# The same steps of an attention and feed-forward kernel in another order

## The chip, the core and the metric

The kernel runs on one core of one Trainium2 chip. Times are device microseconds of one launch. The core has five instruction queues that run beside each other: TensorE (PE, with the weight loads PEld shown apart), VectorE (DVE), ScalarE (ACT), GpSimd (POOL) and SyncE (SP). The last two, and ScalarE at the very end, also issue DMAs. Every queue runs its own instructions strictly in order; across queues they wait for each other by semaphores.

## The reference

A gated linear attention with a running state is followed by a bilinear feed-forward layer. Batch 4, 8 heads, 768 steps, head size 48; all in float32.

```python
for t in range(S):                       # per batch and head
    state = alpha[t][:, None] * state + outer(k[t], v[t])
    y[t] = q[t] @ state
x = y.transpose(0, 2, 1, 3).reshape(B * S, H * D)        # 3072 x 384
out = ((x @ w_a) * (x @ w_b)) @ w_out                    # w_a, w_b: 384 x 1536
```

`w_a` and `w_b` are drawn at random like the other inputs.

## The kernel before

**Chunks.** The work is cut into six chunks (0 to 5). A chunk is two of the four batches, called units u = 0 and 1, times 256 steps; chunks 0 and 1 are the first 256 steps of the two batch pairs, 2 and 3 the next, 4 and 5 the last. Each chunk goes through three stages.

*Preparation.* `ld` loads a (alpha), k, q and v. `ln` takes the logarithm of alpha on ScalarE; `l2`, `l2s`, `R`, `H` and `L` add pairs of steps and split the sums in parts that TensorE can multiply; `B`, `A2` or `AQ` sum them along time by a triangular matrix; `E` takes the exponentials of the sums (`b`: decay, `i`: its inverse); `ra` and `lv` bring the two steps of a pair to one level; `mk` and `mq` write the scaled keys and queries. `dk`, `de` (first chunks) or the DMAs `dr`, `dl` make the decay of the state. `C` and `Ce` turn keys and queries on TensorE and copy them out of PSUM in chunks 0 and 1; later `T`, a transposing DMA on SyncE, and the copy `Tr` do this.

*Attention.* `v` and `vs` lay out the values. `K` and `K2` (L760, L773) form key-value products, `k` (L787 to L791) updates the state, `D` (L805) forms scores, `M` masks them, or `Mc` copies and `Mm` masks afterwards. `SB` and `SA` (L834) add what the state carries over, `Y` (L834) what lies inside the chunk, and `X` (L870, L872) copies the result out.

*Feed-forward.* `a f` and `b f` (L889) are one of twelve 128-column blocks of x @ w_a and x @ w_b: three matmuls of 512 columns for both units (`*`), or of 256 columns for one. `as` (L895) copies the `a` block out of PSUM on ScalarE, into one of three buffers; `pr` (L903) multiplies it with the `b` block on VectorE. `o m h` (L911) is half h of the product with w_out for output tile m; `oc` (L922) does the same for half of the columns. `ot` (L926 on ScalarE, L928 on VectorE) copies the tile out of PSUM, into one of four buffers that are taken in turn, and `st` (L944) stores it by a DMA of SyncE. `W` and `Wo` load the weights in slices by GpSimd DMAs (`W a`, `W b`: w_a, w_b).

**Where the order comes from.** The order is written out in a string, `PROGRAM`, and nothing reorders it. A step is a name with arguments, and ahead of a line stands the chunk it belongs to: in `1: ot 1 V`, tile 1 of chunk 1 is copied out by VectorE. The last letter of many steps says which engine takes it: V VectorE, S ScalarE, P GpSimd, Y SyncE. The last number of a matmul step is the PSUM bank, 0 to 7, where its result goes (`D`, `SB`, `B` and `AQ` take two neighbours). This loop builds the instructions:

```python
    for line in PROGRAM.split("\n"):
        if line.strip():
            c, ops = line.split(":")
            for op in ops.split(";"):
                name, *args = op.split()
                OPS[name](chunks[int(c)], *args)
```

So the position of a step in the string is its position in its engine's queue. A step waits for what it reads, and for the last use of the bank or buffer that it writes. The buffer of an output tile is the one that `ot` took four calls earlier, and the new `ot` waits until the store out of it has landed:

```python
    def ff_out(ch, m, eng):
        ch.ot[m] = wk.tile([128, d_model], F32, name="ot", bufs=4)
        evict(ch.ot[m], ch.pf["o", m], eng)
```

Chunks overlap: while chunk c is in the feed-forward stage, chunk c + 1 is prepared and goes through attention between the feed-forward blocks. The prediction writes steps with the chunk ahead where it is needed, so `0 st 2` is the store of tile 2 of chunk 0.

Of the kernel before, what the change touches and what calls it, by code (L numbers as in the profile page):

```python
# [72 lines left out]
0: cz 1 v P
1: v 0 S
0: as 11 *; c3 P
1: vs 0 1 S
0: b 11 * 1; pr 11 *; b 6 * 2; pr 6 *
# [174 lines left out]
3: b 8 * 1
2: ot 1 V
3: a 8 * 0; as 8 *
5: l2s 1 P
3: a 6 * 2; as 6 *
5: l2s 0 V; ra 0
3: a 2 * 3; a 9 * 0; as 9 *; b 6 * 2
4: T 0; dr
5: l2 0 P  # L260
3: a 3 * 4; pr 8 *
4: vs 1 0 S
5: R 0; R 1; ra 1
4: Tr 0 V; v 0 S
3: pr 6 *
5: lv 1 q P
3: b 9 * 5; pr 9 *; a 1 * 0; b 2 * 1; as 2 *
4: T 1
3: pr 2 *
5: AQ 6; E 1 i  # L270
4: dl; D 0 0 2; M 0 0
3: as 1 *
5: E 0 i
3: as 3 *; b 1 * 5; pr 1 *; a 5 * 1; as 5 *
# [9 lines left out]
3: pr 3 *
4: D 0 1 0
1: st 1 Y
4: vs 0 1 V; D 1 1 4
5: E 1 b
4: D 1 0 6; Mc 1 0
# [3 lines left out]
4: K * 0 2; k * 0 V; M 0 1
5: dr
2: o 3 1 -; ot 3 S
4: vs 0 0 V
3: b 10 * 6; b 4 * 7; pr 4 *
2: st 1 Y
3: b 5 * 2; pr 5 *
4: SB 1 0; SB 0 4  # L300
5: mq 0 V
4: Mm 1 0 V
3: a 7 * 3; as 7 *; a 10 * 7; as 10 *
2: st 3 Y
4: vs 1 1 S
3: o 3 0 2; o 2 0 3; pr 10 *
4: Y 0; SA 0; X 0 S; Mm 1 1 V
5: mk 0 V
# [1 line left out]
4: SA 1; Y 1; X 1 S  # L310
5: T 0; mk 1 V; T 1; v 0 S
3: b 7 * 6; o 0 0 7
4: b 3 * 0
5: vs 0 1 S
3: pr 7 *
4: b 4 * 1
# [5 lines left out]
5: Tr 0 V
4: pr 6 *; as 8 *; b 8 * 3
5: v 1 V; vs 1 1 V
4: pr 8 *; a 0 * 5; as 0 *; a 7 * 6; as 7 *
3: o 3 1 -; ot 3 S; ot 0 V
5: D 0 0 0; Tr 1 V; Mc 0 0; D 1 0 6
4: pr 0 *
5: M 1 0; D 1 1 4; K * 0 3; k * 0 V
3: o 1 0 2; o 1 1 -  # L330
4: a 11 * 3
5: Mc 1 1; SB 0 0; Mm 1 1 V
3: ot 1 V
4: as 11 *
5: D 0 1 4; M 0 1; SB 1 6
4: b 7 * 2; pr 7 *; a 10 * 3; as 10 *
3: st 2 Y
4: b 11 * 4; pr 11 *; a 2 * 2; b 2 * 3; b 1 * 4; a 5 * 5
# [4 lines left out]
5: vs 1 0 S; vs 0 0 P; Mm 0 0 V; Y 0; SA 0; X 0 V
4: as 5 *
5: Y 1
4: b 5 * 3; pr 5 *; b 10 * 5; pr 10 *
5: X 1 S; a 3 * 0; b 10 * 1; b 3 * 3; a 0 * 5; as 0 *
# [721 lines left out]
```

## Time and profile before

| | us |
|---|---|
| median of 3 runs | 191.82 (191.68 to 191.87) |
| the profiled execution | 191.33 |
| its span, first to last instruction | 189.5 |
| TensorE busy | 183.1 (97%) |
| VectorE busy | 135.3 (71%) |
| ScalarE busy | 117.2 (62%) |
| GpSimd busy | 57.7 (30%) |
| granted TensorE clock | 1.00 throughout |

The page lists busy time, the span in 40 slices of 4.7 us each, the chain of waits that ended last, and the costliest groups of instructions with their mean duration. A wait is listed as who waited, for whom, the total, how often and the longest. A timeline row is the start, the duration, the engine, the line, the operation, the tiles and their shapes, and how many instructions were merged; in brackets stands the idle time before it and what ended it. A DMA row of an issuing queue shows how long the issue took, and the DMA view adds the time from issue to landing.

### The profile page before, as it was taken

How to read it: one execution, taken by the hardware profiler on the slowest of the kernel's cores; microseconds unless marked ns; L12 is line 12 of the kernel's file. 1: busy time of each engine (PE TensorE's matmuls, PEld its weight loads, DVE VectorE, ACT ScalarE, POOL GpSimd, SP SyncE). 2: the span in 40 equal slices, each digit the busy share in tenths (PEclk: the TensorE clock that was granted, in tenths of full speed). 3: DMA queues.
4: the chain of work that ended last, by engine and by line, in shares of the span. 5: the costliest groups of instructions: out<-in, count | busy, mean ns of one | idle time of the engine just before them, and what ended most of it. 6: DMA issues, size and time to landing. Idle time of an engine off the chain costs nothing.

```text
span 189.5 us, 6112 instructions
## 1 busy us (share of the span) xinstructions
PE 183.1 (97%) x2597; PEld 114.6 (60%) x2613; DVE 135.3 (71%) x246; ACT 117.2 (62%) x220; POOL 57.7 (30%) x81
## 2 busy tenths in 40 slices
PE   7999899999999999999999999999999999999993
PEld 3888676656688776644457544646446454545563
DVE  2477778679898999797899898995287753144511
ACT  4497586896978996667475979747625524320610
POOL 8999177985154000203930226002000000000000
PEclk9999999999999999999999999999999999999999
DMA  5999999999999799988999396926902100002123
GB/s 130 265 223 199 263 241 248 237 258 268 236 220 194 102 190 263 266 231 154 208 267 206 93 159 134 127 85 71 175 27 83 45 3 0 0 5 83 42 83 125
DMA packets 64475, 29.41 MB, mean 155 GB/s; under 512 B 55760, under 2 KB 62816, under 8 KB 64448
## 3 DMA queue, kind: packets, MB, share of 16 engines
q1 hardware_dynamic: 46080, 16.34, 40.9%
q0 software_dynamic: 18224, 12.58, 38.8%
q8 instruction: 20, 0.33, 0.7%
q10 hardware_dynamic: 144, 0.10, 0.2%
q14 instruction: 7, 0.06, 0.1%
HBM read 25.98 MB, written 4.74 MB: 162 GB/s over the span
## 4 chain that ended last, share of the span: by engine, by line
PE 88%; DMA 4%; DVE 3%; issue 2%; POOL 2%; ACT 1%; POOLq 0%; ACTq 0%
PE psum L889 47%; PE psum L911 24%; PE psum L834 6%; DMA a_t<-in_alpha_dram 4%; PE psum L805 2%; PE psum L704 2%; PE psum L599 1%; DVE prod L903 1%; PE psum L922 1%; PE psum L773 1%; PE psum L760 1%; PE psum L666 1%; PE psum L557 1%; PE psum L558 1%; DVE vx L928 1%
## 5 line engine op out<-in xcount | busy, mean ns | idle before, releaser
L889 PE MATMUL psum<-xT,wb_t 128*128 128x512 bf16 (+1 forms) x261 | 54.7, 335 | 1.1 <-DVE vx L928 0.4
L889 PE MATMUL psum<-xT,wa_t 128*128 128x512 bf16 (+1 forms) x264 | 54.7, 336 | 0.4 <-issue 0.2
L911 PE MATMUL psum<-wo_t,prod 128*128 128x384 bf16 x276 | 49.2, 326 | 0.1
L889 PEld LDWEIGHTS <-wa_t 128*128 128x128 bf16 x270 | 25.8, 98 | 20.1 <-issue 0.2
L889 PEld LDWEIGHTS <-wb_t 128*128 128x128 bf16 x270 | 25.6, 98 | 19.6 <-DMA wb_t<-in_moe_w_b_dram 0.7
L911 PEld LDWEIGHTS <-prod 128*128 128x128 bf16 x276 | 26.2, 98 | 17.9
L926 ACT ACTIVATE ot<-psum 128x384 f32<-128x384 f32 (+1 forms) x12 | 5.7, 478 | 17.9 <-PE psum L911 15.3
L618 POOL TENSOR_TENSOR q_t<-q_t,ra 128x384 f32<-128x384 f32 x7 | 7.0, 1007 | 28.0 <-ACT ra L611 26.9
L926 ACT ACTIVATE vx<-v_t 32x384 bf16<-32x384 bf16 x28 | 14.6, 521 | 0.5
L579 POOL TENSOR_TENSOR l<-la 64x384 f32<-64x384 f32 x6 | 6.0, 994 | 26.0 <-PE psum L889 11.3
L818 ACT ACTIVATE m<-psum 128x768 bf16<-128x768 f32 x14 | 11.0, 810 | 3.2 <-PE psum L805 3.1
L928 DVE COPY ot<-psum 128x384 f32<-128x384 f32 (+1 forms) x13 | 7.0, 536 | 7.5 <-PE psum L911 7.0
L814 DVE TENSOR_TENSOR m<-psum,mask 128x768 bf16<-128x768 f32 x10 | 9.5, 952 | 1.8 <-PE psum L805 1.2
L522 ACT ACTIVATE la<-a_t 128x1536 f32<-128x1536 f32 (+2 forms) x9 | 9.4, 1053 | 2.0 <-DMA a_t<-in_alpha_dram 2.0
L870 ACT ACTIVATE xT<-psum 128x768 bf16<-128x768 f32 x10 | 7.9, 811 | 4.1 <-PE psum L834 3.9
L644 DVE TENSOR_TENSOR QKp<-q_t,beta 128x768 bf16<-128x768 f32 x10 | 9.4, 952 | 0.6 <-POOL q_t L618 0.6
L644 DVE TENSOR_TENSOR QKp<-k_t,invb 128x768 bf16<-128x768 f32 x10 | 9.6, 968 | 0.4 <-ACT invb L633 0.2
L834 PE MATMUL psum<-m,vx 64*64 64x64 bf16 (+1 forms) x576 | 8.7, 205 | 0.0
L515 POOL DMA_DIRECT2D v_t<-in_v_dram x8 | 8.7, 1087 | 0.0
L834 PEld LDWEIGHTS <-vx 64*64 64x64 bf16 x576 | 7.6, 108 | 0.6 <-issue 0.5
L737 ACT ACTIVATE vx<-v_t 128x768 bf16<-128x768 bf16 x9 | 7.5, 838 | 0.3 <-DMA v_t<-in_v_dram 0.2
L822 DVE TENSOR_TENSOR m<-m,mask 128x768 bf16<-128x768 bf16 x14 | 7.4, 551 | 0.4 <-ACT m L818 0.3
(278 smaller groups left out, 300.5 us busy)
## 6 DMA issues: line engine op xcount, KB each, us to landing
out_dram<-ot SPq DMA_DIRECT2D x23, 192.0 KB, 2.0
q_t<-in_q_dram SPq DMA_DIRECT2D x3, 768.0 KB, 6.0
k_t<-in_k_dram SPq DMA_DIRECT2D x3, 768.0 KB, 12.1
a_t<-in_alpha_dram POOLq DMA_DIRECT2D x2, 768.0 KB, 11.9
v_t<-in_v_dram POOLq DMA_DIRECT2D x4, 384.0 KB, 8.2
a_t<-in_alpha_dram SPq DMA_DIRECT2D x2, 768.0 KB, 6.7
...
```

Of the source, the lines that this page charges most:

```text
L515: eng.dma_start(out=t[:, us, hs].rearrange("p b h r d -> p (b h) (r d)"), in_=src[ch.b0 + us.start:ch.b0 + us.stop, hs, ch.s * 2 * C:(ch.s ...
L522: nc.scalar.activation(out=ch.la[:, us, hs].rearrange("p b h r d -> p (b h r d)"), in_=ch.a[:, us, hs].rearrange("p b h r d -> p (b h r d) ...
L644: eng.tensor_mul(QKp[ch.c % 2][:, u, j, :, hs, :D], src[:, u, hs].rearrange("p h r d -> p r h d"), f)
L737: nc.scalar.activation(out=o_, in_=i_, func=AF.Copy)
L814: nc.vector.tensor_mul(m, x, maskn())
L818: nc.scalar.activation(out=m, in_=x, func=AF.Copy)
L834: nc.tensor.matmul(o, lhsT=lhsT, rhs=rhs, start=(g, c) not in begun, stop=False, skip_group_check=True)
L870: nc.scalar.activation(out=o_, in_=i_, func=AF.Copy)
L889: nc.tensor.matmul(p, lhsT=(wa_t, wb_t)[w][:, kk, f * 128:(f + 1) * 128], rhs=ch.xT[:, kk, us, :], start=(kk == 0), stop=(kk == KT - 1))
L911: nc.tensor.matmul(op, lhsT=ch.prod[:, f, at:at + C], rhs=wo_t[:, f, :], start=(f == 0), stop=(f == NFF - 1))
L926: nc.scalar.activation(out=o_, in_=i_, func=AF.Copy)
L928: eng.tensor_copy(o_, i_)
```

## The change

Only `PROGRAM` changes. It holds the same 872 steps before and after, none added and none left out; every matmul, copy, load and store is still there with the same shape. What differs is the order of the steps, the PSUM banks, and for some steps the engine: five `l2s` and one `vs` go from GpSimd to VectorE, three `v` from ScalarE to VectorE and three the other way, `ot` six from ScalarE to VectorE and nine the other way, `X` three and two, `vs` two and five, one `Tr` from VectorE to ScalarE, one `Ce` the other way, `l2` one from GpSimd to VectorE and two the other way, `lv` two each way. The new order is made by the rule that the second slice of w_b (columns 256 to 768) and all loads behind it may land late.

The diff, cut to the start, the stretch from the attention of chunk 1 to the first feed-forward blocks of chunk 2, the output of chunk 2, and the end:

```diff
 1: ld q 0 P
-0: Y 0
+0: SA 0; K 0 1 5; mq 1a V; v 1 S; vs 1 1 S; mk 1a V; C 1 0 0; mk 1b V; K 1 1 1; mq 1b V; X 0 S; C 1 1 6; K 1 0 7; de 1; Ce 1 0 V
 1: ld k 0 P
-0: mk 1a V; SA 0; E 1b b; mq 1a V; mk 1b V; C 1 0 7; K 1 1 2; mq 1b V; Ce 1 0 V; C 1 1 3; v 1 S; Ce 1 1 V; de 1; K 1 0 4; k 1 0 V; k 1 1 V; D 1 0 6; X 0 S
-0: a 2 0 0; a 4 0 1; Mc 1 0; vs 1 1 V; as 4 0; vs 1 0 V; a 5 0 3; D 1 1 4; Mc 1 1; SB 1 6; Mm 1 1 V; a 1 0 1; Mm 1 0 V; b 4 0 2; as 1 0; pr 4 0; a 3 0 4; as 3 0
-0: b 0 0 1; K 0 1 5; SA 1; Y 1; a 0 0 2; as 2 0; b 2 0 0; k 0 1 V; X 1 S; b 3 0 4; pr 3 0
+0: Ce 1 1 V; D 1 0 2; Mc 1 0; a 4 0 0; as 4 0; a 5 0 4; k 1 0 V; k 0 1 V; a 3 0 6; as 3 0; k 1 1 V; vs 1 0 V; SB 1 2; Mm 1 0 V; D 1 1 6; Mc 1 1; a 0 0 5; Mm 1 1 V
+0: a 2 0 0; b 4 0 1; pr 4 0; b 2 0 6; b 3 0 7; as 2 0; pr 2 0; as 5 0
...
-1: C 1 1 2; C 1 0 4
...
+1: mk 1 V; C 1 1 0
+0: ot 2 S
+1: C 1 0 1; M 0 1; Mm 0 0 V; Y 0; SA 0; X 0 S; k 0 1 V
 0: st 3 Y
...
-1: K2 1 1 5 7; Ce 1 0 V; D 1 1 2; Y 0; v 1 S; SA 0
...
+1: K2 1 1 2 3; v 1 V; Ce 1 1 V; D 1 1 4
...
+1: o 3 1 -; ot 3 S; st 3 Y
+2: Mm 1 0 V
+3: lv 0 q V; AQ 6; E 1 b
+2: SA 0
+3: E 0 b
+2: Y 0; X 0 S
+0: st 2 Y
+2: SA 1
+3: lv 0 k V
+2: Y 1
+3: dr; lv 1 q V; mq 1 V
+1: o 1 0 5
+3: mq 0 V
+1: o 1 1 -
+3: E 0 i
+2: X 1 S; b 1 * 6
+4: l2s 0 V
+3: v 0 S
+1: st 2 Y
+3: mk 0 V
+0: cs 0 0 P
+2: b 9 * 0
+3: E 1 i
+4: ra 1; ld q * Y; ra 0; lv 0 q P
+3: vs 0 1 S
+1: ot 1 V
+2: a 11 * 1; a 1 * 7; as 1 *
+3: lv 1 k V; mk 1 V
+2: pr 1 *; a 8 * 5; b 11 * 2
+3: dl
+2: a 5 * 3
+4: l2 0 V
+2: a 9 * 6
+1: ot 0 S
+2: as 11 *; pr 11 *
+3: T 0; T 1
+1: st 0 Y
...
-1: ot 3 S; st 3 Y
-3: ra 0; E 1 b; E 0 b; E 0 i
-2: SA 0
-0: st 2 Y
-1: ot 0 V
-2: Y 1; Mm 0 1 V; SA 1; X 1 S; Mm 0 0 V; Y 0
-3: E 1 i
-1: o 1 0 6; o 1 1 -
-2: X 0 V; a 1 * 7
-3: lv 0 k V; dr
-4: ld q * Y
-3: lv 0 q P; mq 0 V
-2: a 9 * 0; as 1 *
-3: mk 0 V
-2: a 11 * 1; as 11 *; a 8 * 7
-3: lv 1 q V; lv 1 k V; mk 1 V; mq 1 V
-2: b 9 * 2; b 11 * 1; b 8 * 3; pr 11 *
...
-1: ot 1 V; st 2 Y
...
+3: Y 1; X 1 S
+1: st 1 Y
+4: lv 0 k V; mk 0 V
+3: SA 0; Y 0; X 0 S
...
+2: o 1 0 0; o 1 1 -
...
+2: ot 0 S
+3: a 3 * 2
+2: ot 1 S; st 1 Y
...
-5: ot 0 V; o 3 1 -; st 0 Y; o 2 1 -; ot 2 V; ot 3 S; st 3 Y; st 2 Y; oc 1 1 0 0; oc 1 1 1 -; otc 1 1 V; stc 1 1 S; oc 1 0 0 1; oc 1 0 1 -; otc 1 0 S; stc 1 0 Y
...
+5: o 3 0 5; pr 8 *; pr 11 *; o 3 1 -; oc 1 1 1 -; otc 1 1 V
+4: st 2 Y
+5: o 0 1 -; ot 0 V; st 0 Y; ot 3 V; st 3 Y; o 2 1 -; ot 2 S; st 2 Y; oc 1 0 0 1; stc 1 1 S; oc 1 0 1 -; otc 1 0 S; stc 1 0 Y
```

More of the change, by code (lines that the diff above doesn't have):

```diff
@@ new lines @@
+0: a 0 1 1; b 4 1 7
+1: ld q 1 P
+0: as 0 0; Wo 0 6; b 3 1 0; a 1 1 2
+1: lv 0 q P; ld k 1 P
+0: b 0 1 3
+1: lv 0 k P
+0: pr 0 0; a 3 1 4; a 4 1 5; as 0 1; b 1 1 1; pr 0 1; Wo 6 12
+1: H 1 V
+0: as 1 1; pr 1 1
+1: H 0 V; L 0 V
+0: b 2 1 6
+1: L 1 V
+0: a 2 1 2; as 2 1; pr 2 1; as 3 1; pr 3 1; as 4 1
+1: ra 1
+0: a 5 1 3; a 6 * 1; a 8 * 2
+1: A2 0 4
+0: pr 4 1; a 7 * 5; b 7 * 0; as 7 *; a 10 * 6
+2: ld a * P
+0: pr 7 *; b 10 * 5
+1: ld v 1 P
+0: b 5 1 0; as 5 1; pr 5 1
+1: lv 1 q P
+0: b 8 * 3
+1: A2 1 7
@@ L69 @@
+2: ld q * P
+0: as 8 *
+1: E 0 b
+0: as 10 *; pr 10 *; pr 8 *
+1: E 0 i
+0: b 9 * 0
+1: mk 0 V; lv 1 k P; E 1 i
+0: b 11 * 6
+1: mq 0 V
+0: a 11 * 2; as 11 *; pr 11 *; a 9 * 3; as 9 *; b 6 * 4
+1: E 1 b; dk * 5; C 0 0 2; Ce 0 0 V; de *; C 0 1 3
+0: o 2 0 5; as 6 *; pr 6 *
+1: v 0 S; vs 0 1 S; D 0 0 6; Mc 0 0
+0: pr 9 *
 2: ld k * P
-1: de *
-0: b 8 * 0; pr 8 *
+1: K2 0 0 2 4; k 0 0 V; vs 0 0 S
+0: o 3 0 1; o 1 0 0
 3: ld v * P
[L73 to L77, printed above, removed]
@@ new lines @@
+0: cz 1 v P; o 3 1 -; ot 3 S; o 1 1 -; ot 1 S
+2: ln *
+0: o 2 1 -; c3 P
+3: ld a * P
+1: mk 1 V; C 1 1 0
+0: ot 2 S
+1: C 1 0 1; M 0 1; Mm 0 0 V; Y 0; SA 0; X 0 S; k 0 1 V
+0: st 3 Y
+1: K2 1 1 2 3; v 1 V; Ce 1 1 V; D 1 1 4
+0: o 0 0 0
+1: vs 1 1 S; Mc 1 1; a 2 0 6; as 2 0; a 4 0 7; as 4 0
+2: l2 0 P
+1: Ce 1 0 V
+2: l2s 0 V
+0: cs 1 0 P
+2: l2s 1 V; R 0
+1: a 6 0 1; as 6 0; k 1 0 V
+0: o 0 1 -; ot 0 S; st 0 Y
+1: b 2 0 2
+2: R 1; ra 1; lv 1 q P
+1: D 1 0 4; k 1 1 V; M 1 0; pr 2 0
+2: AQ 6
+1: b 6 0 0; b 4 0 1; vs 1 0 S; a 5 0 3
@@ L129 @@
+0: st 1 Y
+1: SB 1 4; pr 6 0
+2: E 0 b; lv 1 k P
+1: pr 4 0
+2: E 1 i; E 1 b
+1: a 10 0 2; as 10 0; b 7 0 0; as 5 0; b 1 0 1
+2: ld v * P
+1: a 1 0 7; as 1 0; b 5 0 2
+2: dr
+1: Mm 1 1 V; b 10 0 3
+2: ra 0; lv 0 q P
+1: Y 1
+2: E 0 i; mk 1 V
+1: pr 1 0; SA 1; X 1 S; a 3 0 7; a 7 0 1; b 8 0 6; pr 10 0; a 8 0 3; b 0 0 4; pr 5 0; as 7 0
+2: mq 1 V
+1: as 3 0; a 0 0 1; b 3 0 2; a 0 1 5; as 8 0; a 11 0 3
 2: mq 0 V
-1: as 3 0
-3: ln *
-1: a 10 1 2; b 10 1 6; b 3 0 7; pr 7 0; as 10 1; pr 10 1; pr 3 0
+1: b 11 0 7; pr 7 0; b 0 1 0; pr 3 0; a 10 1 2; pr 8 0
@@ L251 @@
-4: v 1 S
[L252 to L267, printed above, removed]
-4: T 1
[L269 to L274, printed above, removed]
-5: lv 0 k P
-3: a 4 * 0
-5: E 0 b
+1: as 0 1
+2: lv 0 k P
+1: pr 0 1
+3: ra 0; l2s 0 P
@@ new lines @@
+1: as 10 1; pr 10 1; as 6 1; a 7 1 2; as 11 1
+2: mk 0 V
+1: b 6 1 5; pr 6 1; b 7 1 0; as 7 1
+2: dl
+1: b 11 1 1; a 2 1 2
+2: T 0
+1: b 9 0 6; pr 11 1; o 2 0 7; b 2 1 1
+3: v 1 S
+1: pr 7 1; as 9 0; pr 9 0; as 2 1
+2: Tr 1 S
+3: l2s 1 V
+1: a 4 1 0; as 4 1; pr 2 1; b 4 1 5
+2: K2 * * 6 2
+1: pr 4 1
+2: D 1 0 0
+1: as 9 1
+2: k * 0 V; v 1 S; k * 1 V; Mc 1 0
+1: a 1 1 3
+3: ra 1
+2: vs 1 0 V
+1: b 9 1 4; pr 9 1
+4: ld a * Y
+1: as 1 1
+2: vs 1 1 S
+1: a 3 1 5; as 3 1; o 2 1 -; b 8 1 6
+2: Tr 0 V
@@ new lines @@
+1: b 1 1 0; pr 1 1; a 5 1 1; as 5 1
+2: v 0 V
+1: a 8 1 2; as 8 1; b 3 1 3; pr 3 1
+3: ld q * Y
+1: o 0 0 4; ot 2 S; pr 8 1
+2: vs 0 1 V; D 0 0 0; D 1 1 2; M 1 1
+3: ld k * Y
+4: ld k * Y
+2: Mc 0 0
+1: b 5 1 5; pr 5 1; o 0 1 -
+2: SB 1 0; SB 0 2
+3: R 0; R 1
+2: D 0 1 6
+4: ln *
+2: Mc 0 1; Mm 0 1 V
+1: o 3 0 5
+2: Mm 0 0 V; vs 0 0 S
+1: o 3 1 -; ot 3 S; st 3 Y
[9 more added lines that the diff above has]
+3: dr; lv 1 q V; mq 1 V
@@ new lines @@
+4: lv 1 q V
+2: as 8 *
+3: K2 * * 0 2; k * 0 V; k * 1 V
+2: a 0 * 1; as 0 *
+5: ld a * Y
+2: b 8 * 5; pr 8 *; b 2 * 3; as 2 *; pr 2 *; b 0 * 0; pr 0 *; a 4 * 1; a 7 * 2
+3: Tr 0 S
+2: b 7 * 4; as 7 *; pr 7 *; as 4 *; a 10 * 3; as 10 *
+3: vs 0 0 S
+2: b 4 * 0
+3: Tr 1 V
+2: b 10 * 1; pr 4 *
+4: lv 1 k P
+3: D 1 0 2
+2: pr 10 *
+3: D 0 1 4; Mc 0 1; M 1 0
+4: l2s 1 V; R 0
+3: D 0 0 6; Mc 0 0
+4: R 1
+2: o 2 0 0; o 2 1 -
+5: ld q * Y
+3: SB 0 2; vs 1 1 P; SB 1 4; D 1 1 6
+5: ld k * Y
+3: Mc 1 1; Mm 1 1 V
@@ new lines @@
+2: o 0 0 1; o 0 1 -
+5: ln *; ra 0
+4: AQ 6; E 0 i; ld v * P; E 1 i
+3: SA 1
+4: E 0 b
+2: ot 2 V; st 2 Y
+3: Mm 0 1 V; Mm 0 0 V
+5: l2s 0 V; l2s 1 V
+3: Y 1; X 1 S
+1: st 1 Y
+4: lv 0 k V; mk 0 V
+3: SA 0; Y 0; X 0 S
+4: mq 0 V; T 0
+5: l2 0 V
+2: o 1 0 0; o 1 1 -
+4: E 1 b; dr; mq 1 V
+5: R 0
+2: ot 0 S
+3: a 3 * 2
+2: ot 1 S; st 1 Y
+4: mk 1 V
+3: a 2 * 3; a 8 * 0; a 1 * 1; as 8 *; b 8 * 4; a 11 * 0; as 11 *
+4: v 1 S
+5: R 1
+3: as 2 *; pr 8 *; a 6 * 5; as 6 *; b 11 * 6; pr 11 *; as 1 *
+4: T 1
@@ L278 @@
+3: b 2 * 0; pr 2 *
+5: ra 1
+3: b 1 * 4; a 9 * 3; as 9 *
+5: AQ 0; E 0 i; E 1 b; lv 1 q P
+4: Tr 0 V
+5: lv 0 k P
+4: v 0 S
+3: pr 1 *
+4: D 0 0 6; M 0 0
+3: b 6 * 4
+5: E 0 b; E 1 i
+3: b 9 * 3; b 3 * 5; a 0 * 6; b 0 * 7; pr 6 *; pr 9 *
+4: dl
+3: as 3 *; pr 3 *; as 0 *; a 4 * 0
+4: Tr 1 V; vs 0 1 S
 3: as 4 *
 5: ld v * P
-4: Tr 1 V
-3: b 3 * 2
-2: o 3 0 3; st 2 Y
-5: lv 0 q V
[L284 to L289, printed above, removed]
-5: lv 1 k V
-4: Mc 1 1
-5: mq 1 V
@@ L293 @@
[L293 to L308, printed above, removed]
-2: st 0 Y
[L310 to L316, printed above, removed]
+3: a 5 * 6; as 5 *
+4: vs 1 0 S
+3: pr 0 *
+4: K * 0 1; k * 0 V; D 1 1 2; Mc 1 1; D 0 1 4; M 0 1
@@ new lines @@
+2: o 3 0 0; o 3 1 -; ot 3 V; st 3 Y
+5: lv 0 q V
+4: vs 1 1 S; Mm 1 1 V; SB 0 2; SB 1 4; D 1 0 6
+5: lv 1 k V
+4: Mc 1 0; vs 0 0 S
+3: b 4 * 1; pr 4 *; b 5 * 0; b 10 * 6
+5: v 1 S
+3: a 7 * 7; b 7 * 1; pr 5 *; o 3 0 0
+4: Mm 1 0 V
+3: as 7 *; pr 7 *
+5: mq 1 V
+4: Y 0; SA 0; Y 1; X 0 V; SA 1
+3: a 10 * 1
+5: mk 0 V; dr; mq 0 V
+3: o 2 0 7
+5: v 0 V; vs 0 0 V
+4: X 1 S; a 4 * 2; a 3 * 3; as 3 *; a 0 * 4; b 3 * 5
+5: T 0
+4: a 6 * 3
+3: as 10 *
+4: pr 3 *; a 9 * 1; b 6 * 5
+3: pr 10 *; o 2 1 -
+2: st 0 Y
@@ L317 @@
+4: b 9 * 6
+5: mk 1 V
+4: as 4 *
+3: o 3 1 -; ot 2 V
+4: as 9 *
+5: T 1
+4: pr 9 *
+3: ot 3 V
+5: Tr 0 V
+4: b 4 * 2; pr 4 *; b 0 * 1
+3: o 0 0 0
+4: a 8 * 2; as 6 *; pr 6 *
+5: Tr 1 V
+3: st 2 Y
 5: dl
-4: a 4 * 6; a 3 * 4; as 4 *; pr 4 *; as 3 *; pr 3 *; a 6 * 5
-3: o 2 1 -; ot 2 S
-4: a 9 * 4; as 9 *; a 8 * 6; b 9 * 3; pr 9 *; b 0 * 4; as 6 *; b 6 * 5
+4: a 7 * 3
 3: o 0 1 -
[L322 to L338, printed above, removed]
+4: as 0 *; pr 0 *
+5: D 1 1 4
+4: as 8 *
+3: ot 0 V
+4: as 7 *
+5: vs 1 1 S; D 0 0 2; Mc 0 0; D 1 0 6; M 1 0; K * 0 1
+4: b 7 * 0; pr 7 *; a 5 * 2
+5: Mc 1 1
+4: b 8 * 3
+5: k * 0 V
+4: pr 8 *; a 11 * 0; as 11 *
@@ L339 @@
+3: o 1 0 4; o 1 1 -
+5: D 0 1 0; M 0 1
+4: as 5 *
+5: SB 1 2; SB 0 6
+3: ot 1 S
+4: a 1 * 5; as 1 *; b 5 * 4
+5: Mm 0 0 V
+4: b 1 * 0; pr 1 *; b 11 * 5; a 10 * 1; b 2 * 0
+5: vs 1 0 S; Mm 1 1 V; Y 1; SA 1
+4: pr 5 *
+5: vs 0 1 S; Y 0; SA 0; X 0 S
+4: a 2 * 4
 3: st 3 Y
-4: as 2 *; pr 2 *; a 1 * 2
-5: SA 1
+4: pr 11 *; b 10 * 5
+5: X 1 V; a 2 * 2; as 2 *; b 1 * 3; b 2 * 6
 3: st 0 Y
[L343 to L347, printed above, removed]
@@ L364 @@
[L364 to L367 removed]
+5: pr 2 *; a 9 * 2
+4: as 2 *
+5: b 9 * 4; b 7 * 6; a 0 * 7
+4: as 10 *
+5: a 4 * 1; as 9 *; pr 9 *; b 0 * 2
+4: pr 2 *; pr 10 *; o 0 0 0; o 0 1 -; ot 0 S
+5: b 4 * 4; b 3 * 5; as 0 *; pr 0 *
+4: o 1 0 0; o 1 1 -
+5: as 4 *; a 1 * 1; as 1 *; pr 1 *; pr 4 *; a 3 * 7; as 3 *; pr 3 *; b 5 * 2; a 5 * 1; a 7 * 3
```

210 lines of the change are left out of this document (19 added, 191 removed).

## The prediction

> **What bounds the kernel now.** I read the page from the top: engine shares, the 40 slices, the chain that ended last. These are lines of the page:
>
> ```profile
> span 189.5 us, 6112 instructions
> PE 183.1 (97%) x2597; PEld 114.6 (60%) x2613; DVE 135.3 (71%) x246; ACT 117.2 (62%) x220; POOL 57.7 (30%) x81
> ...
> PEclk9999999999999999999999999999999999999999
> DMA  5999999999999799988999396926902100002123
> ...
> PE 88%; DMA 4%; DVE 3%; issue 2%; POOL 2%; ACT 1%; POOLq 0%; ACTq 0%
> ```
>
> TensorE is busy 97% of the span at the full granted clock, and the chain lies 88% on it. The change keeps TensorE's matmuls, so it can gain only what TensorE now idles, and lose by every new wait of TensorE. So next I read TensorE's waits. After the first matmuls at 11.6 us there is one real one, seen in the waits of the weight loads (11.6 to 30 us) and in TensorE's timeline:
>
> ```profile
> PEld L889 <- DMA wb_t<-in_moe_w_b_dram: 0.7, 1, 0.7
> ```
>
> ```profile
> 19.64 0.50 PE L889 MATMUL psum<-xT,wa_t 128*128 128x256 bf16 x3
> 20.57 0.50 PE L889 MATMUL psum<-xT,wb_t 128*128 128x256 bf16 x3 [0.43 <-DVE vx L928]
> ```
>
> `b 4 0`, the first block on w_b, waits for the slice 256 to 768 of w_b (issued at 13.24, landed 7.3 us later, at 20.5). The rest of TensorE runs without a gap, so the question is where the new order makes it wait. To find that, I went through the new order block by block, laid the durations of the groups end to end on each engine, and asked when a block's inputs and its PSUM bank come free and when TensorE wants them. Nearly everywhere the bank is free some 0.3 us ahead, as before. One place stands out, and it hangs on SyncE's queue. Its timeline, then the DMA view of 79.3 to 79.5 us:
>
> ```profile
> 65.45 0.97 SPq L515 DMA_DIRECT2D a_t<-in_alpha_dram  x1
> 66.52 2.20 SPq L515 DMA_DIRECT2D q_t<-in_q_dram  x1
> 68.82 7.51 SPq L515 DMA_DIRECT2D k_t<-in_k_dram  x2
> 77.01 2.67 SPq L944 DMA_DIRECT2D out_dram<-ot  x2
> ```
>
> ```profile
> DMA packets 162, 0.06 MB, mean 311 GB/s; under 512 B 162, under 2 KB 162, under 8 KB 162
> ...
> out_dram<-ot SPq DMA_DIRECT2D x1, 192.0 KB, 4.1
> ```
>
> SyncE issues four loads of 768 KB in a row (`4 ld a`, `3 ld q`, `3 ld k`, `4 ld k`) and then two stores, `1 st 3` and `0 st 2`. The second store is issued at 79.26; the bytes then moving are all packets under 512 B, the loads', and the store lands 4.1 us later, at 83.4, where the median of all 23 stores is 2.0. What used that store in VectorE's timeline:
>
> ```profile
> 79.55 0.56 DVE L618 TENSOR_TENSOR k_t<-k_t,a_t 128x384 f32<-128x384 f32 x1
> 80.03 0.95 DVE L644 TENSOR_TENSOR QKp<-q_t,beta 128x768 bf16<-128x768 f32 x1
> ...
> 91.69 0.53 DVE L928 COPY ot<-psum 128x384 f32<-128x384 f32 x1
> ```
>
> The last line is `1 ot 1`: it refills the output buffer that `0 st 2` empties (four buffers, taken in turn). Before, it comes 8.3 us after the landing and never waits.
>
> **The change part by part.** Durations are of this one execution: 191.33 us, span 189.5 and 1.8 around it; the median of the three runs, 191.82, is 0.5 above it.
>
> *The wait for w_b.* `b 4 0` now follows five blocks of w_a and the key-value product `K 0 1` (0.36 us), so it comes near 21.1, after the landing at 20.5: the 0.43 goes. Late next is bank 6: `a 3 0` is put there and `D 1 1` wants banks 6 and 7, after `as 3 0` has emptied it. ScalarE gets there later, because two half-height copies (`vs 1 1`, 0.52 each) and `X 0` (0.8) now stand before `de 1`, `Mc 1 0` (0.8), `as 4`, `as 3` (0.3 to 0.4 each): from 15.6, where `v 1` starts (0.8), these add to 20.1. TensorE is there at 19.6: 18.08, where the first w_a block starts now, plus 0.36, three blocks of 0.33 and `SB` 0.15. ScalarE's instructions overlap by up to 0.1, so +0.3 to +0.5; I take +0.4. Net 0.
>
> *Switches between full-array and quadrant matmuls.* A lone `SB` between feed-forward blocks costs 0.48, inside a longer group 0.15; two `D` cost 0.69, three 0.95, so going in and out costs 0.17 to 0.33. The new order joins `C 1 1`, `C 1 0` with the group `Y 0`, `SA 0`, `K2 1 1`, `D 1 1` (1.00 and 1.39 apart): -0.25. `K 0 1` leaves the group at 21.65, where it cost 0.6 with 0.20 idle, for a run of its own kind: -0.2. `SA, Y, SA, Y` after the cumulative sum cost 2.27 in chunk 2 and `Y, SA, Y, SA` 2.41 in chunk 3; chunk 3 now has the former: -0.14. In all -0.45 before 82 us, -0.14 after; between -0.2 and -0.8.
>
> *The store's wait.* TensorE begins the fifth chunk-2 block at 82.96. In the new order the fifth is `a 8` in bank 5, where `o 1` of chunk 1 was summed, and `1 ot 1` on VectorE has to empty bank 5 first. So `a 8` starts after the landing of `0 st 2` plus 0.53. SyncE's order up to it is the same. With the landing at 83.4, `1 ot 1` ends at 83.95 and `a 8` starts at 84.0: +1.05 against 82.96, whatever was gained before, since the gains only bring TensorE to this wait earlier. The landing can itself come sooner, by what the loads start sooner: they follow the transposes and `mk 0` of chunk 2, which the 0.45 gained brings forward, so 0 to 0.6; then `a 8` starts at 83.4 to 84.0. I take the middle, 83.7: +0.75. Behind `1 ot 1` stand on VectorE `lv 1 k` (0.55), `mk 1` (0.95), `pr 1` (0.73): with 0.1 overlap bank 6 comes free 2.1 us after, TensorE wants it for `a 9` three blocks (1.94) later: +0.1.
>
> VectorE is late before this too: it now reaches `lv 0 k` of chunk 3 near 77, and `3 ld k` lands near 78.2 (an estimate: `4 ld a` lands 6.7 after 65.45, then two loads of 0.79 MB at the 261 GB/s of that stretch). From there `lv 0 k`, `lv 1 q`, `mq 1`, `mq 0`, `l2s 0`, `mk 0` are 4.1 us in a row, to 82.3. So a store that landed at once would still leave `a 8` at 82.9.
>
> *Everything else.* Engines swapped: five `l2s` go from GpSimd (0.99) to VectorE (0.55), `vs`, `v`, `ot`, `X`, `Tr` swap between VectorE and ScalarE; net VectorE +0.8, ScalarE +3.8, GpSimd -5. TensorE's 97% hides it, as VectorE idles 54 us and ScalarE 72; without that cover it would cost 4. GpSimd's DMAs keep their order: 0. SyncE: `1 st 2` goes ahead of `4 ld q` (0.9 later, landing 88.0, first used at 90.16): hidden. `1 st 0` goes ahead of chunk 5's loads and `2 st 2`, `1 st 1` come behind them, ahead of `4 T 0`: third rival. The end: one half column of the last tile moves forward; the last store is again 96 KB after 12 matmuls of 192 columns (0.99) and a 0.33 copy, but `st 2` is issued 0.9 nearer: 0 to +0.3, I take 0.
>
> **Sum.** +0.75 +0.1 -0.14 = +0.7 against the profiled 191.33, so 192.0 there, and 192.5 against the median 191.82. Its own range, with `a 8` at 83.4 to 84.0 and the other bounds, is +0.3 to +1.4: 192.1 to 193.2.
>
> **The rivals.**
>
> *Faster: load and store land in time.* TensorE is at the fifth block at 82.5, so `1 ot 1` must start by 81.9: `0 st 2` has to land 1.5 us sooner than before and `3 ld k` by 77.8, 0.4 sooner. For it: most stores take 2.0 us, and the loads may start up to 0.6 sooner. Against: 4.1 here and 5.6 for `0 st 0` at 51.15, both behind loads. Then only the gains stand: -0.45 -0.14, 191.2.
>
> *No change.* The store takes the median 2.0 and lands at 81.3, or at least by 82.6, but VectorE comes late from `3 ld k`: `a 8` starts at 82.9 to 83.2, and with -0.14 behind it that is -0.2 to +0.1: 191.6 to 191.9. Against it stands the same 4.1. The Trainium skill ("DMA: Bandwidth & Descriptors", Anatomy of one DMA) speaks for it: a transfer has a fixed cost of about 2 us, most of it the receipt of the write, by which alone `0 st 2` would land near 81.3, an estimate from that page. This store's 4.1 differs; the same page (Queues, rings and completion order) says that a ring's descriptors are consumed in order, and the packets under 512 B after 79.3 agree with that.
>
> *A second store's wait.* After chunk 5's loads, `1 st 0` took 5.03 us to issue at 96.84. `2 st 2` and `1 st 1` now stand there, and `ot 1` of chunk 2 on ScalarE needs the buffer of `1 st 1`, near 106.7; `5 ld k` lands 12.1 after 94.02, at 106.1. So 0 to +0.6 on top; +0.4 gives 192.9.
>
> **How the numbers follow.** Forecast 0.47, second wait 0.17, no change 0.16, faster 0.20. This kernel can't be told from unchanged within about 0.2% (0.38 us): slower 0.64, same 0.16, faster 0.20. The range reaches from the faster case's 191.2 to 193.3, where the second wait's bound ends; that leaves out about half of the faster case and some of the slowest.
>
> **What would show it.** After: no wait of `b 4` for w_b near 21 us, a short one of `D 1 1` before it; in VectorE's timeline an idle stretch ahead of the `ot` copy near 83 us, put down to the store or to ScalarE, and TensorE waiting for `1 ot 1` at its fifth chunk-2 block. If TensorE has no gap near 83 us, the forecast is wrong and the first rival right; a gap near 107 us shows the third rival.

## The result, and the profile after

The changed kernel takes 194.03 us (median of 6 runs, 193.85 to 194.16); the kernel before, beside it, 192.03. The ratio is 1.0100, with a 95% interval from 1.0069 to 1.0131: slower by about 1.9 us. The forecast was 192.5 with a range of 191.2 to 193.3, so the direction came true and the size lies outside the range. Ratios here are taken over undisturbed runs alone, so they need not equal the quotient of the medians. The profiled execution after is 193.96 us, span 192.2. The line numbers of the changed kernel are lower by one than before, because its program string has one line less; those of the kernels below differ by up to two.

The page, with the lines that answer to those of before:

```profile
span 192.2 us, 6122 instructions
PE 185.4 (96%) x2613; PEld 115.2 (60%) x2613; DVE 136.3 (71%) x244; ACT 120.5 (63%) x228; POOL 53.7 (28%) x75
...
PE   7999899999999999969999999999999999999993
...
PE 91%; DVE 4%; ACT 3%; issue 1%; DVEq 0%; ACTq 0%
```

TensorE's row of the 40 slices is full but for the ends and one "6", in the slice from 81.7 to 86.5 us. The chain held 3% VectorE and 1% ScalarE before; both shares are larger now. TensorE's waits name the place (who waited, for whom, total, how often, longest):

```profile
PE psum L888 <- DVE ot L927: 1.7, 1, 1.7
...
PE psum L888 <- issue: 0.3, 1, 0.3
PE psum L804 <- ACT as__486 L894: 0.2, 1, 0.2
```

The wait of `b 4 0` for the w_b slice is gone and `D 1 1` waits 0.2 for `as 3`, both as forecast (the latter at 0.3 to 0.5). The 1.7 is `a 8`, the fifth chunk-2 block. TensorE's timeline there, and VectorE's beside it:

```profile
82.30 1.46 PE L888 MATMUL psum<-xT,wa_t 128*128 128x512 bf16 x6
85.41 0.81 PE L888 MATMUL psum<-xT,wa_t 128*128 128x512 bf16 x3 [1.66 <-DVE ot L927]
```

```profile
77.70 0.55 DVE L617 TENSOR_TENSOR q_t<-q_t,ra 128x384 f32<-128x384 f32 x1
80.36 0.56 DVE L617 TENSOR_TENSOR k_t<-k_t,a_t 128x384 f32<-128x384 f32 x1 [2.10 <-DMA k_t<-in_k_dram]
80.83 0.55 DVE L617 TENSOR_TENSOR q_t<-q_t,ra 128x384 f32<-128x384 f32 x1
81.49 1.83 DVE L643 TENSOR_TENSOR QKp<-q_t,beta 128x768 bf16<-128x768 f32 x2
83.35 0.55 DVE L578 TENSOR_TENSOR l<-la 64x384 f32<-64x384 f32 x1
83.93 0.96 DVE L643 TENSOR_TENSOR QKp<-k_t,invb 128x768 bf16<-128x768 f32 x1
84.81 0.55 DVE L927 COPY ot<-psum 128x384 f32<-128x384 f32 x1
```

`a 8` does wait for `1 ot 1`, at the forecast place. But `1 ot 1` (84.81) follows `mk 0` without idle time: no store holds it. What holds VectorE is `lv 0 k`, which stands 2.10 for the load `3 ld k`, landing at 80.3. With `lv 1 q`, `mq 1`, `mq 0`, `l2s 0` and `mk 0` behind it, that is 4.45 us of work in a row, and `1 ot 1` ends at 85.36. So the first theory after the result was the *load theory*: the load and VectorE's order make the stall. Its rival was the forecast's *store theory*.

To see where time goes besides, I compared the two traces at the points where both orders have issued the same set of matmul steps (the blocks of one width counted alike). The table gives how much later than in the trace of before the next step starts (its first weight load), for the changed kernel and four of the kernels below. Each column is one execution, so its level at the top differs from execution to execution; the last section says by what. The rows are points where both orders go on with a step of the same kind, except 85.64, where a change of kind shifts the new order's lag by a few tenths.

| at (us of before) | changed | e1 | e9 | e8 | e5 |
|---|---|---|---|---|---|
| 6.11 | +0.35 | +0.33 | +0.18 | -0.56 | -0.24 |
| 15.87 | +0.26 | +0.13 | +0.12 | +0.58 | +0.82 |
| 23.32 | +0.30 | +0.37 | +0.30 | +0.94 | +1.18 |
| 77.04 | +0.44 | +0.51 | +0.43 | +1.08 | +1.38 |
| 82.75 | +0.63 | +0.50 | +0.43 | +1.07 | +1.38 |
| 83.40 | +2.45 | +0.50 | +1.60 | +1.49 | +1.38 |
| 85.64 | +2.36 | +0.28 | +1.52 | +1.78 | +2.69 |
| 106.22 | +2.48 | +0.31 | +1.70 | +1.86 | +3.17 |
| 106.81 | +2.47 | +1.52 | +1.69 | +1.86 | +3.17 |
| 185.75 | +2.48 | +1.52 | +1.70 | +1.87 | +3.18 |

In the changed kernel 1.82 of 2.48 come between 82.75 and 83.40, and nothing after 107.

### The profile page after: what moved, and what is told of

It is laid out like the page before. It is cut to its first block, busy times and chain, and to the rows that moved or that the text cites. A ratio compares the mean times of both kernels' runs of the same rounds, so it can differ in the third digit from the quotient of the medians.

```text
span 192.2 us, 6122 instructions
## 1 busy us (share of the span) xinstructions
PE 185.4 (96%) x2613; PEld 115.2 (60%) x2613; DVE 136.3 (71%) x244; ACT 120.5 (63%) x228; POOL 53.7 (28%) x75
## 4 chain that ended last, share of the span: by engine, by line
PE 91%; DVE 4%; ACT 3%; issue 1%; DVEq 0%; ACTq 0%
PE psum L888 47%; PE psum L910 23%; PE psum L833 5%; PE psum L804 3%; PE psum L703 2%; DVE QKp L643 2%; PE psum L539 2%; PE psum L556 2%; PE psum L557 2%; PE psum L665 1%; PE psum L598 1%; PE psum L759 1%; PE psum L921 1%; PE psum L772 1%; ACT xT L869 1%
## 5 line engine op out<-in xcount | busy, mean ns | idle before, releaser
L888 PE MATMUL psum<-xT,wa_t 128*128 128x512 bf16 (+1 forms) x270 | 55.7, 337 | 1.7 <-DVE ot L927 1.7
L888 PE MATMUL psum<-xT,wb_t 128*128 128x512 bf16 (+1 forms) x270 | 55.8, 337 | 0.3 <-issue 0.3
L617 POOL TENSOR_TENSOR q_t<-q_t,ra 128x384 f32<-128x384 f32 x6 | 6.4, 1072 | 54.1 <-ACT ra L610 27.6
L925 ACT ACTIVATE vx<-v_t 32x384 bf16<-32x384 bf16 x34 | 17.7, 521 | 0.6
L925 ACT ACTIVATE ot<-psum 128x384 f32<-128x384 f32 (+1 forms) x15 | 7.2, 482 | 16.3 <-PE psum L910 15.6
L643 DVE TENSOR_TENSOR QKp<-k_t,invb 128x768 bf16<-128x768 f32 x10 | 10.3, 1030 | 0.2
L869 ACT ACTIVATE xT<-psum 128x768 bf16<-128x768 f32 x9 | 7.2, 815 | 5.2 <-PE psum L833 5.1
L927 DVE COPY ot<-psum 128x384 f32<-128x384 f32 (+1 forms) x10 | 5.3, 534 | 5.6 <-PE psum L910 3.3
L833 PE MATMUL psum<-kqT,Sm 64*64 64x128 bf16 x144 | 7.6, 218 | 0.0
## 6 DMA issues: line engine op xcount, KB each, us to landing
out_dram<-ot SPq DMA_DIRECT2D x23, 192.0 KB, 2.8
```

The source lines that it names most:

```text
L643: eng.tensor_mul(QKp[ch.c % 2][:, u, j, :, hs, :D], src[:, u, hs].rearrange("p h r d -> p r h d"), f)
L833: nc.tensor.matmul(o, lhsT=lhsT, rhs=rhs, start=(g, c) not in begun, stop=False, skip_group_check=True)
L869: nc.scalar.activation(out=o_, in_=i_, func=AF.Copy)
L888: nc.tensor.matmul(p, lhsT=(wa_t, wb_t)[w][:, kk, f * 128:(f + 1) * 128], rhs=ch.xT[:, kk, us, :], start=(kk == 0), stop=(kk == KT - 1))
L925: nc.scalar.activation(out=o_, in_=i_, func=AF.Copy)
```

## The experiments

Every kernel was run beside the kernel before. Single runs of one of them lie up to 2.1 us apart, of the kernel before up to 3.7, so ratios with their 95% intervals are compared.

**e1: the late step behind the copy.** From the changed kernel:

```diff
-3: lv 0 k V
 2: Y 1
...
-3: mk 0 V
 0: cs 0 0 P
...
 1: ot 1 V
+3: lv 0 k V; mk 0 V
```

> The changed kernel (194.0), with chunk 3's lv 0 k and mk 0 moved on VectorE from their places ahead of 1 ot 1 to right behind it. Load theory (the fifth chunk-2 block a 8 waits because VectorE stands 2.1 us at lv 0 k for the load 3 ld k, landing 80.3, and then has 4.4 us of work before 1 ot 1): VectorE reaches 1 ot 1 near 81.7, the wait of 1.66 of a 8 goes; lv 0 k, mk 0, lv 1 k, mk 1 (3.0) now stand between 1 ot 1 and pr 1, so a 9 in bank 6 may wait up to 0.5; time 192.3 to 192.9. Store theory (the prediction: 1 ot 1 waits for the landing of 0 st 2, estimated 83.4 to 84): 1 ot 1 shows idle time ended by the store's DMA, a 8 starts at 84.0 to 85.3, and the time falls by 0 to 1.4 only, 192.6 to 194.0.

Measured: 192.25, ratio 1.0008 (0.9984 to 1.0032); the changed kernel has 1.0100. VectorE's timeline, then the DMA view of 81.2 to 81.75 us:

```profile
80.60 0.55 DVE L577 TENSOR_TENSOR l<-la 64x384 f32<-64x384 f32 x1
81.18 0.56 DVE L926 COPY ot<-psum 128x384 f32<-128x384 f32 x1
81.66 0.55 DVE L616 TENSOR_TENSOR k_t<-k_t,a_t 128x384 f32<-128x384 f32 x1
```

```profile
DMA packets 183, 0.21 MB, mean 379 GB/s; under 512 B 71, under 2 KB 182, under 8 KB 182
```

`1 ot 1` now runs at 81.18, with no wait, and `a 8` follows its neighbours without a gap: +0.50 on both sides of 83.40 in the table. The store `0 st 2` was issued at 79.98. From 81.2 until the next store is issued at 81.75, 111 packets of between 512 B and 2 KB still move (182 less 71), the size of a store's rows, and the semaphore that `0 st 2` raises has its last update at 84.35. If `1 ot 1` refilled the buffer of `0 st 2`, it could not have started at 81.18. The addresses in the built program say why: `1 ot 1` has the buffer of `0 ot 1`, whose store `0 st 1` landed at 57.2. The description above and the prediction have the buffers taken strictly in turn, and they are not; in the kernel before, too, `1 ot 1` has another buffer than `0 ot 2`, that of `1 ot 3`. The store theory falls at its root.

The mended order uncovers another wait, 1.21 between 106.22 and 106.81. In TensorE's waits it is the first line here:

```profile
PE psum L887 <- ACT xT L868: 1.0, 1, 1.0
PE psum L803 <- ACT xT L868: 0.5, 1, 0.5
```

`X 1` of chunk 3 was late because the logarithm `5 ln *` stands ahead of it on ScalarE and started late. Its row in ScalarE's timeline in e1, and in e4 below:

```profile
103.20 1.49 ACT L520 ACTIVATE la<-a_t 128x1536 f32<-128x1536 f32 x1 [1.61 <-DVE m L820]
```

```profile
102.59 1.49 ACT L521 ACTIVATE la<-a_t 128x1536 f32<-128x1536 f32 x1 [0.72 <-DMA a_t<-in_alpha_dram]
```

In e1 the profile names a mask step of VectorE that comes behind `5 ln *` in the order and so can't hold it; in e4 it names the load `5 ld a`, and in e1 that load's semaphore has its last update at 103.12, just ahead of `5 ln *`. The changed kernel gets there 2 us later and does not wait.

**e2: e1 with a fifth output buffer** (`bufs=5` in both places that allocate one).

> The kernel of e1_k_behind with five output buffers instead of four, so that 1 ot 1 waits for no store. It prices the store alone. Load theory: same time as e1_k_behind within 0.3, since the store had landed. Store theory: faster than e1_k_behind by the idle time that 1 ot 1 showed there, 0.5 to 1.5.

Measured: 192.11, ratio 0.9986 (0.9960 to 1.0011), no difference from e1 shown: a wait for a store's buffer plays no part here.

**e4: the late step on another engine.** From the changed kernel:

```diff
-3: lv 0 k V
+3: lv 0 k P
```

> The changed kernel (194.0) with one letter changed: chunk 3's lv 0 k on GpSimd instead of VectorE. GpSimd then takes the wait for 3 ld k (landing 80.3); mk 0 stays ahead of 1 ot 1 on VectorE and needs lv 0 k. Load theory: VectorE does lv 1 q, mq 1, mq 0, l2s 0 meanwhile (to 81.2), mk 0 starts when GpSimd is done at about 81.4, 1 ot 1 ends near 83.0, and a 8 is wanted at 83.4: its wait of 1.66 goes, time 192.2 to 192.5. Rival (the work ahead of 1 ot 1 on VectorE is what counts, not where the load is waited for): VectorE still has the wait, now in mk 0, and a 8 waits 0.7 or more; 193.0 or more.

Measured: 192.04, ratio 0.9993 (0.9966 to 1.0020). The first line is GpSimd's timeline, the second VectorE's:

```profile
80.60 1.08 POOL L617 TENSOR_TENSOR k_t<-k_t,a_t 128x384 f32<-128x384 f32 x1 [16.78 <-DMA k_t<-in_k_dram]
```

```profile
83.00 0.55 DVE L927 COPY ot<-psum 128x384 f32<-128x384 f32 x1
```

One letter takes the whole loss away, to just below the 192.2 to 192.5 expected: GpSimd, with nothing else to do, waits for the load, and `1 ot 1` starts 1.8 us sooner, though `mk 0` still stands ahead of it.

**e5: only the copy sooner.** From the changed kernel:

```diff
+1: ot 1 V
 4: l2s 0 V
...
 3: vs 0 1 S
-1: ot 1 V
```

> The changed kernel with 1 ot 1 moved on VectorE ahead of l2s 0 (chunk 4) and mk 0 (chunk 3); lv 0 k with its wait for the load, lv 1 q, mq 1 and mq 0 stay ahead of it. A half dose: 1.5 of the 4.4 us of work between the landing and 1 ot 1 go. Load theory: lv 0 k starts at 80.3 again, 1 ot 1 ends at 83.85 instead of 85.35, a 8 waits 0.2 to 0.5 instead of 1.66: time 192.6 to 192.9. Store theory (already unlikely by e1_k_behind): 1 ot 1 would stand for the store.

Measured: 193.83, ratio 1.0087 (1.0058 to 1.0116). This was a miss: 192.6 to 192.9 was expected. TensorE's timeline shows why:

```profile
83.05 2.10 PE L888 MATMUL psum<-xT,wa_t 128*128 128x512 bf16 x9
...
87.90 2.10 PE L888 MATMUL psum<-xT,wa_t 128*128 128x512 bf16 x9 [1.45 <-DVE prod L902]
```

`a 8` no longer waits, but `a 9`, three blocks on, waits 1.45 for `pr 1`, which stands behind the same VectorE queue. Moving the copy moved the stall. The load theory had to be sharpened: VectorE's queue as a whole loses the time that it stands at `lv 0 k`, and whichever of its steps frees the next bank passes the delay to TensorE.

**e8: the copy on ScalarE**, which tests that.

```diff
-1: ot 1 V
+1: ot 1 S
```

> The changed kernel with 1 ot 1 on ScalarE instead of VectorE; nothing else moves. After e5_ot_sooner the theory is sharper: the stall belongs to VectorE's queue as a whole, which loses about 2 us at lv 0 k, and whatever stands behind it releases its bank late. Theory queue: a 8 no longer waits (ScalarE is free near 83 and lets bank 5 go by 84), but a 9 waits for pr 1, the next VectorE step that frees a bank; VectorE ends pr 1 only 0.55 sooner than in the changed kernel, near 86.9, and a 9 is wanted at 85.9: a wait of 0.8 to 1.2, time 193.2 to 193.6. Rival (only the place of 1 ot 1 counts): 192.2 to 192.5.

Measured: 193.18, ratio 1.0049 (1.0020 to 1.0078). TensorE:

```profile
84.45 0.81 PE L888 MATMUL psum<-xT,wa_t 128*128 128x512 bf16 x3 [0.26 <-ACT ot L925]
...
87.00 2.10 PE L888 MATMUL psum<-xT,wa_t 128*128 128x512 bf16 x9 [0.44 <-DVE prod L902]
```

The wait moves on to `a 9` and `pr 1` as the sharpened theory says, and the time is slightly below the 193.2 to 193.6 expected. `a 8` still waits 0.26, for ScalarE, where no wait was expected. `pr 1` ends at 86.94, as expected, but the wait of `a 9` is smaller than its 0.8 to 1.2, because TensorE gets there 0.7 later than assumed: by the 0.26, and because this execution was 0.4 later than the changed kernel's ahead of the stall (table, 82.75).

**e3 and e9: the load sooner.** Both put steps of chunk 2 and 3 from GpSimd back on VectorE. e3 moves only `2: lv 0 k`; e9 also this:

```diff
-2: lv 0 k P
+2: lv 0 k V
...
-3: ra 0; l2s 0 P
+3: ra 0
...
 2: mk 0 V
+3: l2s 0 V
```

> The changed kernel with chunk 2's lv 0 k on VectorE again (0.55) instead of GpSimd (1.00). Theory GpSimd (this swap and mk 0, which took 1.68 beside GpSimd instead of 0.95, made the transpose T 0 0.95 later, and with it the loads behind it): T 0 is issued near 63.6, 3 ld k lands 0.8 sooner at 79.5, a 8 waits 0.8 less, time 193.2. Rival (the loads' landing is set by the rate of the DMA engines and not by when they are issued, or T 0 waits for something else): a 8 waits as before, 194.0 within 0.3.

> The changed kernel with chunk 2's lv 0 k and chunk 3's l2s 0 on VectorE instead of GpSimd, l2s 0 behind mk 0 of chunk 2, so that GpSimd does nothing beside mk 0; chunk 3's order on VectorE is left alone. A dose for the landing of 3 ld k. Theory load: mk 0 takes 0.95 instead of 1.68 and T 0 is issued 0.8 to 1.0 sooner against TensorE's work; 3 ld k lands 0.6 to 1.0 sooner against it, and a 8 waits 0.7 to 1.2 instead of 1.82 behind the new order's lag; time 193.0 to 193.5. Rival (the landing does not follow T 0): 194.0 within 0.3.

Measured: e3 193.70, ratio 1.0076 (1.0046 to 1.0106); e9 193.27, ratio 1.0069 (1.0039 to 1.0099). In e3 `T 0` is issued at 64.27, hardly sooner by the clock than the changed kernel's 64.38, because TensorE was 0.6 later there; the load lands at 80.2 again, the wait of `a 8` shrinks from 1.66 to 1.2 mostly by that lateness, and 193.70 is the edge of the rival's range. So e3 decides nothing. e9 shows the mechanism; first the changed kernel's VectorE and GpSimd, then e9's SyncE, VectorE and TensorE:

```profile
62.64 1.68 DVE L643 TENSOR_TENSOR QKp<-k_t,invb 128x768 bf16<-128x768 f32 x1
```

```profile
61.44 0.99 POOL L617 TENSOR_TENSOR k_t<-k_t,a_t 128x384 f32<-128x384 f32 x1
62.51 0.99 POOL L578 TENSOR_TENSOR l<-la 64x384 f32<-64x384 f32 x1
```

```profile
63.65 3.00 SPq L713 DMA_TRANSPOSE kqT<-QKp  x1
```

```profile
62.64 0.95 DVE L644 TENSOR_TENSOR QKp<-k_t,invb 128x768 bf16<-128x768 f32 x1
...
79.52 0.56 DVE L618 TENSOR_TENSOR k_t<-k_t,a_t 128x384 f32<-128x384 f32 x1 [1.42 <-DMA k_t<-in_k_dram]
```

```profile
84.57 0.81 PE L889 MATMUL psum<-xT,wa_t 128*128 128x512 bf16 x3 [1.02 <-DVE ot L928]
```

Without GpSimd beside it `mk 0` takes 0.95 instead of 1.68, `T 0` is issued at 63.65 instead of 64.38, the load lands at 79.5 instead of 80.3, and `a 8` waits 1.02 instead of 1.66. That is as expected, but for `T 0`, which gained 0.73 and not 0.8 to 1.0. The load follows the transpose here, though not one for one in every execution (in e8 `T 0` is issued at 65.02, and the load lands at 80.2). The swap to GpSimd was not free, but it is a minor part of the loss: the intervals of e9 and the changed kernel overlap, so the gain is shown by the trace and not by the time.

**e6: e1 with `5 ld a` issued between the transposes `T 0` and `T 1` of chunk 3.**

> The kernel of e1_k_behind with the load 5 ld a issued between the transposes T 0 and T 1 of chunk 3 instead of behind T 1 and 1 st 0. In the profile of e1_k_behind ScalarE stood 1.61 for 5 ld a at 103.2, X 1 came late and TensorE idled 1.04 before 107.9. Theory (a second late load, uncovered once the first is mended): that wait goes, median 191.3 to 192.0 and a smaller spread than 191.6 to 193.2. Rival (T 1 lands later behind the load, and the copy Tr 1 or D 1 0 of chunk 3 waits for it near 97 to 100): no gain, 192.2 or more, with a new gap near 100.

Measured: 196.19, ratio 1.0208 (1.0174 to 1.0242): the rival was right, and the loss is larger than any number that it named. VectorE's wait, then TensorE's timeline:

```profile
DVE kp L927 <- DMA kqT<-QKp: 2.9, 1, 2.9
```

```profile
100.53 1.08 PE L804 MATMUL psum<-kqT,kp 64*64 64x128 bf16 x48 [2.29 <-DVE kp L927]
101.54 3.37 PE L910 MATMUL psum<-wo_t,prod 128*128 128x384 bf16 x12
```

`T 1` behind 768 KB of load lands so late that `Tr 1` waits 2.9 and `D 1 0` of chunk 3 2.3. The loss does not end there: behind this gap the granted clock of TensorE is 0.50 from 101 to 104 us, and the next 12 matmuls take 3.37 instead of 2.12 (e1). TensorE's lag grows by 2.4 at the gap and by 1.5 behind it.

**e10: e4 with `5 ld a` just ahead of `1 st 0`,** both behind the transposes.

> The kernel of e4_lv_gps with the load 5 ld a issued just ahead of 1 st 0 instead of behind it, both behind the transposes. A try for a version faster than both. ScalarE waited 0.7 for 5 ld a near 103 in e4_lv_gps; it lands 0.5 to 0.9 sooner, which saves TensorE 0 to 0.3: median 191.7 to 192.0. Rival (the landing is set by the transposes and loads that share the DMA engines until then): no change from e4_lv_gps, 192.0.

Measured: 191.96, ratio 0.9981 (0.9952 to 1.0009). In its profile `5 ln *` starts at 101.19 without waiting, so the load ahead of the store does land in time. It is the best version found, but 192.0 was the rival's number too, and no difference from e4 or from the kernel before is shown.

**e7: the start of the change by itself.** In the kernel before, `K 0 1` goes ahead of `b 4 0`:

```diff
-... Mm 1 0 V; b 4 0 2; ...
-0: b 0 0 1; K 0 1 5; SA 1; ...
+... Mm 1 0 V; K 0 1 5; b 4 0 2; ...
+0: b 0 0 1; SA 1; ...
```

> The kernel before with one step moved: K 0 1 of chunk 0 ahead of b 4 0 instead of behind b 0 0. It prices by itself what the prediction took for the start of the change: the wait of b 4 0 for the w_b slice (0.43) shrinks by the 0.36 of K 0 1, and K 0 1 no longer opens the quadrant group in front of SA 1. Prediction's terms: -0.36 and -0.2 plus one more switch in and out of 0.17 to 0.33 for the lone K 0 1, in sum -0.2 to -0.4: 191.6 to 191.9 beside a before of 192.0. If the landing of the slice moves about between runs by more than that, no difference.

Measured: 191.93, ratio 0.9999 (0.9977 to 1.0021): no difference shown, though the interval of 0.4 us either way could hide the 0.2 to 0.4 expected. TensorE:

```profile
20.93 0.43 PE L760 MATMUL psum<-v_t,QKp 64*64 64x48 bf16 x16 [0.32 <-ACT m L818]
```

The wait of `b 4 0` went, and `K 0 1` now waits 0.32 for bank 5, which ScalarE's `Mc 1 1` has to empty. Even so the trace gains: TensorE's lag against before is 0.47 ahead of this stretch and 0.23 behind it. At 29.4 it grows by 0.18 again, where a weight load waits 0.29 for the last slice of w_b, landed at 29.3 in this execution and at 28.8 in that of before.

**h2: the new order's first 430 steps, then the rest in the old order.**

> The new order up to D 0 1 of chunk 2 (its first 430 steps, to about 75 us), and behind it the remaining steps in the order of before. It prices the first 75 us of the change alone. By the prediction's sum this part gains 0.45 (switches of TensorE): 191.3 to 191.6. By the lag of the two traces at 75 us (+0.4 at equal TensorE work) it loses 0.4: 192.2 to 192.6. If the load is later with the new front (landing 80.3 instead of at most 79.5), lv 0 k of chunk 3 waits here too, but with no block of TensorE behind it, so no gap over 1 us near 85.

Measured: 195.66. It prices nothing: in this mix `AQ` of chunk 3 writes bank 4 while tile 0 of chunk 1 stands there uncopied, so that tile is lost, and waits arise that neither order has. The table's upper rows answer its question instead.

## Why the prediction was wrong in size and in cause

- **What bounds it, and the place: right.** TensorE bounds the kernel, and the loss came in one stall of `a 8` on `1 ot 1` in bank 5, near 84 us. That the forecast had the direction as well is partly luck: it priced the stall by a store that nobody waits for, and its own account of VectorE without that store, `a 8` at 82.9, gave no loss.
- **"The store's wait": wrong, the step that failed.** Its premise, that `1 ot 1` refills the buffer of `0 st 2`, is false (e1). What the runs show in its place stands in the same part's last lines as a floor: "a store that landed at once would still leave `a 8` at 82.9". That floor was the cause: `lv 0 k` holds VectorE 2.10 for the load, and `a 8` stands 1.66 for it. e1 and e4 give the whole loss back without touching a store, and e2 gains nothing by a fifth buffer.
- **Its landing of `3 ld k`, 78.2: mis-sized by 2.1; measured 80.3.** With 80.3 the same working, at its own 4.1 and 0.53, gives 84.9; the six steps from `lv 0 k` to `mk 0` took 4.45 and not 4.1, which makes it 85.3, and `a 8` started at 85.41. Of the 2.1, 1.3 stood in the trace of before already: there the semaphore that `3 ld k` raises has its last update at 79.46, just ahead of `lv 0 k` at 79.55. The estimate divided bytes by a mean rate. By the 384 B packets counted over all engines, the three loads up to `3 ld k` were through at 71.4, 74.4 and 77.5 there, but they land 0.8, 0.8 and 1.9 after their share of the count (in the changed kernel 1.0, 1.1 and 2.1 after 71.9, 75.0 and 78.2). The other 0.8 came with the new order. "0 to 0.6 sooner" had the wrong sign: `T 0` came 0.95 later (64.38 against 63.43), 0.73 of it, by e9, from the swap to GpSimd.
- **"+0.1 for `a 9`": hidden** in the changed kernel behind the stall of `a 8`; it becomes a whole stall where `a 8` is freed alone (e5: 1.45).
- **The wait for w_b, net 0, and -0.2 for `K 0 1`: right only where no other wait comes up.** `D 1 1` waits 0.19 in every new trace, less than the 0.3 to 0.5. In e10 the lag falls by 0.23 from 15.87 to 23.32, about the -0.2 expected, and e7 gains 0.24 by the move of `K 0 1` alone. But the lag grows by 0.04 in the changed kernel and by 0.18 to 0.64 in the other executions with the new front, by waits that the prediction does not name: `D 1 0` waits 0.2 to 0.6 for `X 0` in seven of the ten, `b 4 0` waits 0.30 for the w_b slice again in e9, where it lands at 21.7, and in five, the changed kernel among them (0.30 at 22.17), TensorE stands 0.3 to 0.6 inside the blocks of w_b, put down to nothing visible. What that last wait is stays open.
- **Switches, -0.25 for joining `C` with `Y`: wrong.** Across the joined stretch, from 43.3 to 52.6 us, the lag of every column grows by 0.01 to 0.02, so nothing is gained. The likely reason is that `C` is itself full-array, so the switch to quadrants remains behind it. TensorE's timeline of the changed kernel has the tile size (128\*128 against 64\*64) in each row:

```profile
46.38 1.06 PE L703 MATMUL psum<-ident,QKp 128*128 128x128 bf16 x16
47.37 0.72 PE L833 MATMUL psum<-m,vx 64*64 64x128 bf16 x48
```

  From 23.32 to 77.04 all columns lose 0.13 to 0.20. The -0.14 for `SA, Y` in chunk 3 is an upper bound: around 103 us the lag falls by 0.14 in e1, 0.10 in e8, 0.07 in the changed kernel and not at all in e9.
- **"Everything else hidden": wrong for the GpSimd swaps** (e9), right for the reordered stores and for the end, where the lag is flat.
- **The rivals.** The second store's wait did not appear: +2.48 at 106.22 and +2.47 behind it. "No change" was right that the store plays no part, though for another reason than a landing after 2 us: `0 st 2` took 3.9 in the changed kernel (80.00 to 83.86), and nobody waits for it. It gave VectorE's lateness at most 0.2. "Faster" needed `3 ld k` at 77.8.

That the table's total (2.48) exceeds the difference of the medians (about 1.9) is because the profiled execution of before, 191.33, was faster by 0.5 to 1.0 than the medians of before in the four sets of runs.
